# Query projection by halves of w_q, keys turned two blocks at a time, and one V load with uneven rows

## The chip, the cores and the metric

One Trainium2 chip, and one of its cores. The metric is device time in microseconds (us) of one execution of the whole kernel. Each NeuronCore has five engines that run side by side and wait for each other by semaphores: PE (TensorE, matmuls; PEld is its weight load), DVE (VectorE), ACT (ScalarE), POOL (GpSimd) and SP (SyncE, which here issues every transfer). Transfers from HBM to the on-chip memory (SBUF) run on 16 DMA engines.

## What is computed

Two layers of a decoder for four sequences with one new token each (x is 4 x 512), and each layer is an attention over cached keys and values and then a gated feed-forward block. Both layers read the same weights and the same caches. Cut to its core:

```python
# B=4, D=512, Hq=32, Hkv=8, Sk=8192, Dh=128, F=1792, all bf16
def attention(x, k_cache, v_cache, wq, wo):      # caches: B x Hkv x Sk x Dh
    q = (x @ wq) as B x Hq x 1 x Dh
    k, v = each of the 8 heads repeated for 4 query heads
    p = softmax(q @ k^T * Dh ** -0.5)
    return (p @ v) as B x 1 x 4096 @ wo
def ffn(x, w_gate, w_up, w_down):
    return (silu(x @ w_gate) * (x @ w_up)) @ w_down
for layer in range(2):
    x = x + attention(layernorm(x), ...)
    x = x + ffn(layernorm(x), ...)
```

## The kernel before

The caches of one layer are 128 MB. The kernel cuts them into 16 units, one per sequence and pair of key heads; a unit has 4 MB of keys (K) and 4 MB of values (V), each laid on 128 partitions (rows) of 32 KB. A row has 8 blocks of 4 KB (`NB = 8`, `BW` is the width of a block). Five slots of that size hold them: slots 0 to 3 and slot 4 (`QS`), whose place w_q has at the start of each layer. The second layer starts with units whose data the first has left in SBUF: K and V of unit 15 and V of unit 14 stay, and the last two blocks of K of unit 13 are parked in PSUM (`hold`) and brought back.

**Order of loads.** `cmds` (lines 349 to 364) is a fixed list of (what, slot, first block, last block). `pump` (L400) goes through it in order and issues the next load when all of its blocks are free; `freed` (L434) marks blocks as free when the step that reads them last has been written, and calls `pump`. All loads go through SP, which waits for the readers of the blocks before it issues (`load`, L419; L63 is the wait and L93 the issue in the profile). Most loads are a whole slot. Some are cut: `half` gives two of four blocks, `ends` gives blocks 0-3, 4-6 and 7. The first loads of layer 1 are K of its second unit (unit 14) into the slot where the feed-forward weights of layer 0 lie (slot 1, as blocks 0-2, 3 and 4-7, each when the weights there have been read), K of the third unit (unit 13) into slot 4 (blocks 0-3, 4-5), and then, from `seq`, K and V of the next, the first two in halves.

**Work on a unit.** `keys` (L598) turns each block of K on DVE (`turn`, L483, transpose on L488: 128 x 1024 fp32, in place) and then writes the scores of the block: four matmuls of 128 x 512 on PE (`scores`, L512). Then come the maximum (L518, L526), the exponentials on ACT (L559), the transpose of the probabilities (L576), and with V the products (`values`, L643), the gather on DVE (L689, L693) and the sums. Work of the next units is placed in between: the order of the instructions on each engine is written out by `blocks`, `line` and `drain`, with a rough cost for each step (0.9 for a block).

**The boundary between layers.** After the last V of layer 0: output projection (L784), layernorm (`center`, L807 to L821; `deviation`, L826), feed-forward (`ffn`: gate and up on L876, down on L907 for layer 0 in three parts of w_down, L897 for layer 1), layernorm again, and the query projection (`qproj`, L839). `qproj` has 128 matmuls of 4 columns: for each of the 32 heads four, over the four parts kt of w_q, of which two come from each half (`wq0`, `wq1`); `deviation` is written after half of the heads. Then `hold` brings the two parked blocks back into slot 4, and blocks 0-5 of slot 4 are freed.

**The end.** V of the last unit comes as blocks 0-3, 4-6 and 7. Behind it come the feed-forward weights of layer 1, and the last part of w_down when the place of the last probabilities is free.

Of the kernel before, what the change touches and what calls it, by code (L numbers as in the profile page):

```python
# [9 lines left out]
FP32 = mybir.dt.float32  # L10
# [93 lines left out]
def bass_interleave_layers__gqa_block_cached__swiglu_ffn__decode_kernel(  # L104
# [40 lines left out]
    with ExitStack() as es:  # L145
# [50 lines left out]
        def room(s, a, b):  # L196
            return [f"s{s}.{q}" for q in range(a // BW, (b - 1) // BW + 1)]
# [48 lines left out]
        def bank(k):  # L246
            return ps[:, k * BANKF:(k + 1) * BANKF]
# [87 lines left out]

        ends = lambda it, s: [(it, s, 0, QH), (it, s, QH, NB - 1), (it, s, NB - 1, NB)]
        half = lambda it, s: [(it, s, q, q + NB // 2) for q in range(0, NB, NB // 2)]

        def placed(seq, ring, parts):
            out = []  # L340
            for i, it in enumerate(seq):
                s = ring[i % len(ring)]
                out += parts[i](it, s) if i in parts else [(it, s, 0, NB)]
            return out
# [10 lines left out]

        us = order[1]
        s = W_SLOT[0]
        cmds += [(K(1, us[1]), s, 0, 3), (K(1, us[1]), s, 3, 4), (K(1, us[1]), s, 4, NB)]
        cmds += [(K(1, us[2]), QS, 0, NB // 2), (K(1, us[2]), QS, NB // 2, NB - 2)]
        seq = loads(1, 3)  # L360
        ring = (0, 1, 3, QS, 2)
        cmds += placed(seq, ring, {0: half, 1: half, len(seq) - 1: ends})
        assert W_SLOT[1] == ring[len(seq) % len(ring)]
        cmds += [(("W", 1), W_SLOT[1], 0, NB), (("W+", 1), W_SLOT[1], NB, NB + 1)]

# [55 lines left out]

        q_gone = set()

        def load(it, a, b, sm):
            kind, L, u = it
            s = slot_of[it]
            gp, bt = pair_gb(u)
            src = (A_k_cache if kind == "K" else A_v_cache)[bt, 2 * gp:2 * gp + 2, :, :].rearrange(
                "h (p t) d -> (h p) (t d)", t=TT)
            over = WQ if s == QS and not q_gone else []  # L430
            q_gone.update(over)
            T.dma("sp", kv[:, s, a * BW:b * BW], src[:, a * BW:b * BW], sm,
                  writes=[f"s{s}.{q}" for q in range(a, b)] + over)

        def freed(s, a, b):
            free.update((s, q) for q in range(a, b))
# [7 lines left out]
        def hold(q, back):  # L444
            s = QS if back else slot_of[half_kept]
            w = kv[:, s, q * BW:(q + 1) * BW].bitcast(FP32)
            k = STEP + 2 * (q - NB + 2)
            banks = ps[:, k * BANKF:(k + 2) * BANKF]
            here, there = [f"s{s}.{q}"], [f"pb{k}", f"pb{k + 1}"]
            if back:  # L450
                T._wait("dve", T._need((), WQ))
                T.op("dve", lambda e: e.transpose(w, banks), reads=there, writes=here)  # L452
                turned.add((1, NP - 3, q))
            else:
                T.op("dve", lambda e: e.transpose(banks, w), reads=here, writes=there)
            held[0] = not back or q < NB - 1
# [23 lines left out]
                line.pop(0)[2]()  # L480


        def turn(L, u, q):  # L483


            s = slot_of[K(L, u)]
            w = kv[:, s, q * BW:(q + 1) * BW].bitcast(FP32)
            T.op("dve", lambda e: e.transpose(w, w), reads=[f"s{s}.{q}"], writes=[f"s{s}.{q}"])  # L488
            turned.add((L, u, q))

        placed_q = set()

# [105 lines left out]
        def keys(L, u, before, lag):  # L598
            def block(q):
                if q == 0:  # L600
                    place_q(L, u)
                scores(L, u, q)
                finished(K(L, u), q, q + 1)
                if q == NB - 1:
                    step = lambda gap, fn: [gap, u, lambda: fn(u)]
                    line.extend([step(0.0, max_p), step(1.2, max_t)])
                    after = [step(0.9, exps), step(1.3, lambda u: turn_p(L, u))]
                    if u == order[L][-1]:
                        after = [after[0], step(0.3, lambda u: turn_p(L, u)), [2.5, None, lambda: total(u)]]
                    (line if before is None else behind.setdefault(before, [])).extend(after)  # L610

            drain(lag)
            for q in range(NB):
                if (L, u, q) not in turned:
                    turn(L, u, q)
                blocks.append((0.9, lambda q=q: block(q)))
                drain(lag)

# [213 lines left out]

        def qproj(L, u):
            at, name = place("ln", 0, Hq * B)
            for h in range(Hq):
                if h == Hq // 2:
                    deviation(lsc_sb, "lsc")
                for kt in range(KT):
                    T.op("pe", lambda e: e.matmul(at[:, h * B:(h + 1) * B],  # L839
                                                  lhsT=wq_sb[:, kt, h * Dh:(h + 1) * Dh],  # L840
                                                  rhs=xn[:, kt * B:(kt + 1) * B],
                                                  start=(kt == 0), stop=(kt == KT - 1)),
                         reads=[f"wq{kt // 2}", "xn"], writes=[name], sig=(kt == KT - 1))
            T.op("dve", lambda e: e.tensor_tensor(qT, at.rearrange("p (h b) -> p b h", b=B),
                                                  rstd[:].unsqueeze(2).to_broadcast([P, B, Hq]), ALU.mult),
                 reads=[name, "rstd"], writes=["qT"] + OT)

            pick = ident.rearrange("p (c j e) -> p c j e", c=2, e=2)
            ob, oname = place("q", 0, NQR)
            ob = ob.rearrange("p (c b g r) -> p c b g r", c=4, b=B, g=GP)  # L850
            qv = qT.rearrange("p b (g h r) -> p b g h r", h=2, r=REP)
            for c in range(4):
                for a in range(NA):
                    T.op("pe", lambda e: e.matmul(ob[a * QB:(a + 1) * QB, c],
                                                  lhsT=pick[:, c // 2, :, c % 2],
                                                  rhs=qv[:, :, :, a // 2, :], start=True, stop=True),
                         reads=["qT", "ident"], writes=[oname], sig=(a == NA - 1))
            place_q(L, u, "dve", ob, [oname])
            T.op("dve", lambda e: e.tensor_copy(qr, ob), reads=[oname], writes=["qr", "made"])

        def ffn(L):
# [3 lines left out]
            uT = bank(ub)[:, 0:FO * B]  # L865
            fb = lambda ap: ap.rearrange("p (f b) -> p f b", b=B)
            rb = rstd[:].unsqueeze(1).to_broadcast([P, FO, B])
            rooms = {"wg": room(s, 0, O_WU), "wu": room(s, O_WU, O_WD), "wd": room(s, O_WD, O_WD + FO * D)}
            names = {"wg": ["wg"], "wu": ["wu0", "wu1", "wu2"]}
            for at, wname, bk in ((wg_at, "wg", gb), (wu_at, "wu", ub)):  # L870
                for fo in range(FO):
# [19 lines left out]
            if L == 1:  # L891
                x_rows(1)
                for i, (a, b, _) in enumerate(WDS[1]):
                    for fo in range(a, b):
                        for j in range(NA):
                            o = s * SL + O_WD + fo * D + j * P
                            T.op("pe", lambda e: e.matmul(quarter(j), lhsT=hT[:, fo * B:(fo + 1) * B],  # L897
                                                          rhs=kvf[:, o:o + P], start=False, stop=(fo == FO - 1)),
                                 reads=["hT", f"wd{i}"] + rooms["wd"], writes=[f"part{j}"],
                                 sig=(fo == b - 1))  # L900
                freed(s, 4, NB)
                return
            for j, (a, b, _) in enumerate(WDS[0]):
                k = OBK[0] if j else SBK[1]
                for nt in range(KT):
                    for fo in range(a, b):
                        T.op("pe", lambda e: e.matmul(bank(k)[:, nt * B:(nt + 1) * B],  # L907
                                                      lhsT=wd_at(s, fo, nt),
                                                      rhs=hT[:, fo * B:(fo + 1) * B],
                                                      start=(j < 2 and nt == 0 and fo == a),  # L910
                                                      stop=(j in (0, NW - 1) and nt == KT - 1 and fo == b - 1)),
                             reads=["hT", f"wd{j}"] + rooms["wd"], writes=[f"pb{k}"], sig=(fo == b - 1))
                if not j:
                    add_to_x(bank(k)[:, 0:XB], f"pb{k}")
            freed(s, 4, NB)
            add_to_x(bank(k)[:, 0:XB], f"pb{k}")


# [10 lines left out]
        for L in range(2):  # L929
# [6 lines left out]
            if L:  # L936
                for q in (NB - 2, NB - 1):
                    hold(q, True)
                freed(QS, 0, NB - 2)
            todo = [("K", 0)]  # L940
            for i in range(1, NP - 1):
                todo += [("K", i), ("V", i - 1)]
# [49 lines left out]
```

## Time and profile before

| | us |
|---|---|
| median of 3 runs | 648.85 (648.73 to 649.52) |
| the profiled execution | 648.29 |
| its span, first to last instruction | 646.5 |
| busy in the span: PE | 425.6 (66%) |
| DVE | 430.1 (67%) |
| ACT | 41.2 (6%) |
| POOL | 11.1 (2%) |
| transfers | 273.37 MB, mean 423 GB/s |

The page of the profile gives busy times, the span in 40 slices of 16.2 us (a digit is the busy share in tenths; GB/s is what the DMA engines moved), the DMA queues, and groups of instructions by line: how often, how long in total, the mean in ns, and then how long the engine was idle just before them and what ended most of that idle time. A row of the timeline has the start, the time, engine, line, operation, output and input, how many instructions were merged, and in brackets the idle time before it and who ended it. The chain of waits follows the work that ended last back from the end of the kernel. q1 is the queue of the kernel's own transfers; q8 carries the program's instructions.

### The profile page before, as it was taken

Reading aid. Unit: us, or ns where it says so; the run is one execution under the profiler, and the core shown is the slowest. Engines: PE = TensorE matmul, PEld = TensorE weight load, DVE = VectorE, ACT = ScalarE, POOL = GpSimd, SP = SyncE. Lnnn points to the kernel's source line nnn. Section 1 sums busy time; section 2 is a strip of 40 time slices with the busy share of each in tenths; the row PEclk is TensorE's granted clock in tenths of the full one; section 3 lists DMA queues with packets and bytes.
Section 4 is the critical chain, followed back from the end, with each engine's and each line's share of the span. In section 5 each row is a group of like instructions: output and inputs, shape, how many; then the busy total and the mean of one; then the engine's idle time right before and its main releaser. Section 6 shows DMA issues by size and latency. Waiting matters only on the chain.

```text
span 646.5 us, 7503 instructions
## 1 busy us (share of the span) xinstructions
PE 425.6 (66%) x3128; PEld 173.1 (27%) x3128; DVE 430.1 (67%) x706; ACT 41.2 (6%) x117; POOL 11.1 (2%) x43
## 2 busy tenths in 40 slices
PE   2574466556766755767757987777665576657878
PEld 2221122212322212222226332222222222222225
DVE  1585467566776666777852878888766677766953
ACT  1000000000000000001010010000000000000110
POOL 0000000000000000000000000000000000000000
PEclk9996896789787999878985799999878997789977
DMA  9999999999999999999999999999999999999996
GB/s 363 445 423 416 442 429 430 426 435 433 426 430 435 430 425 436 435 422 436 434 407 409 396 435 434 434 429 423 442 427 426 433 438 424 431 440 423 430 417 268
DMA packets 14129, 273.37 MB, mean 423 GB/s; under 512 B 1416, under 2 KB 1424, under 8 KB 5264
## 3 DMA queue, kind: packets, MB, share of 16 engines
q1 hardware_dynamic: 14096, 272.91, 99.0%
q8 instruction: 24, 0.39, 0.2%
q14 instruction: 9, 0.07, 0.0%
HBM read 272.90 MB, written 0.00 MB: 422 GB/s over the span
## 4 chain that ended last, share of the span: by engine, by line
DMA 61%; DVE 26%; PE 9%; issue 3%; SPq 0%; ACT 0%; DVEq 0%
DMA kvf<-in_A_k_cache_dram 49%; DVE kvf L488 20%; DMA kvf<-in_A_v_cache_dram 10%; PE ps L512 3%; DVE pT L576 3%; PE ps L643 2%; DMA kvf<-in_B_w_down_dram 2%; DVE pb L693 2%; PE ps L839 1%; DVE pb L689 0%; PE ps L876 0%; DVE scr L703 0%; DVE kvf L452 0%; PE ps L759 0%; SPq L93 0%
## 5 line engine op out<-in xcount | busy, mean ns | idle before, releaser
L512 PE MATMUL ps<-kvf,zq 128*128 128x512 bf16 x1024 | 298.0, 426 | 181.1 <-DVE kvf L488 174.3
L488 DVE STREAM_TRANSPOSE kvf<-kvf 128x1024 f32<-128x1024 f32 x246 | 289.8, 1219 | 108.6 <-DMA kvf<-in_A_k_cache_dram 107.7
L512 PEld LDWEIGHTS ps<-kvf,zq 128*128 128x128 bf16 x1024 | 90.6, 105 | 350.9 <-DVE kvf L488 257.8
L643 PE MATMUL ps<-kvf,pT 128*32 128x512 bf16 x960 | 66.7, 400 | 1.4 <-DVE pT L576 0.8
L559 ACT ACTIVATE pb<-ps,tiny 128x512 bf16<-128x512 f32 x32 | 22.0, 688 | 531.8 <-DVE tiny L557 495.2
L576 DVE STREAM_TRANSPOSE pT<-pb 64x512 bf16<-64x512 bf16 x60 | 41.2, 687 | 3.1 <-ACT pb L559 2.0
L518 DVE TENSOR_REDUCE tiny<-ps 128x1 f32<-128x512 f32 x32 | 22.0, 687 | 31.6 <-PE ps L512 31.6
L693 DVE SCALAR_TENSOR_TENSOR pb<-ps,tiny,pb 128x128 f32<-128x128 f32 x104 | 36.5, 351 | 5.1 <-PE ps L643 1.3
L643 PEld LDWEIGHTS ps<-kvf,pT 128*32 128x32 bf16 x960 | 20.8, 98 | 31.9 <-issue 15.7
L698 PEld LDWEIGHTS ps<-sel,pb 128*128 128x128 f32 x64 | 15.4, 258 | 21.3 <-DVE pb L693 14.0
L502 POOL TENSOR_TENSOR zq<-scr,tiny 128x64 bf16<-128x64 bf16 x30 | 9.0, 300 | 564.8 <-PE ps L512 564.8
L526 DVE TENSOR_REDUCE mrm<-ps 1x8 f32<-1x128 f32 x32 | 8.8, 275 | 14.2 <-PE ps L523 14.2
L698 PE MATMUL ps<-sel,pb 128*128 128x8 f32 x64 | 12.7, 272 | 8.1 <-DVE pb L693 8.1
L549 PEld LDWEIGHTS ps<-mrm,tiny 128*128 128x128 f32 x60 | 12.0, 205 | 8.6 <-DVE scr L703 3.2
L759 PE MATMUL ps<-wo_sb,scr 128*4 128x512 bf16 x48 | 11.0, 379 | 1.5 <-DVE scr L728 1.5
L689 DVE TENSOR_SCALAR pb<-ps,tiny 128x128 f32<-128x128 f32 x32 | 10.1, 315 | 2.6 <-PE ps L643 2.6
L549 PE MATMUL ps<-mrm,tiny 128*128 128x16 f32 x60 | 9.3, 231 | 3.1 <-ACT mrm L561 3.1
L839 PE MATMUL ps<-xn,kvf 128*128 128x4 bf16 x256 | 7.6, 166 | 3.8 <-DMA kvf<-in_A_wq_dram 3.0
L561 ACT ACTIVATE mrm<-head,tiny 128x8 f32<-128x8 f32 x32 | 9.6, 301 | 1.0
L523 PE MATMUL ps<-identf,tiny 128*1 128x128 f32 x32 | 8.6, 270 | 0.2 <-DVE tiny L518 0.2
L839 PEld LDWEIGHTS ps<-xn,kvf 128*128 128x128 bf16 x256 | 7.6, 106 | 4.0 <-DMA kvf<-in_A_wq_dram 3.1
L876 PE MATMUL ps<-xn,kvf 128*128 128x4 bf16 x224 | 7.3, 169 | 1.8 <-DMA kvf<-in_B_w_up_dram 1.4
(83 smaller groups left out, 113.9 us busy)
## 6 DMA issues: line engine op xcount, KB each, us to landing
kvf<-in_A_k_cache_dram SPq DMA_DIRECT2D x28, 4096.0 KB, 30.8
kvf<-in_A_v_cache_dram SPq DMA_DIRECT2D x27, 4096.0 KB, 32.9
kvf<-in_A_v_cache_dram SPq DMA_DIRECT2D x4, 2048.0 KB, 20.0
kvf<-in_A_k_cache_dram SPq DMA_DIRECT2D x4, 2048.0 KB, 10.0
kvf<-in_A_wq_dram SPq DMA_DIRECT2D x2, 2048.0 KB, 9.8
wo_sb<-in_A_wo_dram SPq DMA_DIRECT2D x4, 1024.0 KB, 40.6
kvf<-in_B_w_gate_dram SPq DMA_DIRECT2D x2, 1792.0 KB, 24.5
kvf<-in_A_v_cache_dram SPq DMA_DIRECT2D x2, 1536.0 KB, 34.8
```

The costliest lines, as they stand in the source:

```text
L488: T.op("dve", lambda e: e.transpose(w, w), reads=[f"s{s}.{q}"], writes=[f"s{s}.{q}"])
L512: T.op("pe", lambda e: e.matmul(bank(bk)[:, 0:SW], lhsT=zq[:, z0:z0 + P], rhs=w[:, :, c // 2, :, c % 2], start=(q == 0 and c == 0), stop=( ...
L518: T.op("dve", lambda e: e.tensor_reduce(mx[:], bank(bk)[:, 0:SW], AX.X, ALU.max), reads=[f"pb{bk}"], writes=["mx"])
L549: T.op("pe", lambda e: e.matmul(at, lhsT=ones, rhs=mrm[:, i * H2:(i + 2) * H2], start=True, stop=True), reads=[f"m8{i}", "rsm", "onesf"], ...
L559: T.op("act", lambda e: e.activation(pb[:], bank(bk)[:, 0:SW], ACTF.Exp, bias=nm, accum_out=rs), reads=[f"pb{bk}", "nm"], writes=PB + ["rs"])
L576: T.op("dve", lambda e: e.transpose(dst, pb[hp]), reads=["pb", "row"], writes=[name])
L643: T.op("pe", lambda e: e.matmul(bank(k)[j * QB:(j + 1) * QB, q0 * Dh:q1 * Dh], lhsT=p_t[:, t, h, :], rhs=v[:, q0:q1, t, :], start=((last o ...
L689: T.op("dve", lambda e: e.tensor_scalar(into, o, own[:, q:q + 1], None, op0=ALU.mult), reads=[f"pb{k}", "own"], writes=["row"] if last els ...
L693: T.op("dve", lambda e: e.scalar_tensor_tensor(into, o, own[:, q:q + 1], into, op0=ALU.mult, op1=ALU.add), reads=[f"pb{k}", "own", iname], ...
L698: T.op("pe", lambda e: e.matmul(at, lhsT=into, rhs=sel[:], start=True, stop=True), reads=[iname, "sel"], writes=[name])
L759: T.op("pe", lambda e: e.matmul(bank(OUTB)[0:B, 0:D], lhsT=oT[:, h, :], rhs=wo_sb[:, h, :], start=(gp == groups[L][0] and r == 0), stop=(g ...
L839: T.op("pe", lambda e: e.matmul(at[:, h * B:(h + 1) * B], lhsT=wq_sb[:, kt, h * Dh:(h + 1) * Dh], rhs=xn[:, kt * B:(kt + 1) * B], start=(k ...
```

## The change

1. `qproj` runs over the two halves of w_q outside and the heads inside; `deviation` stands between the halves. In layer 1, blocks 0-3 of slot 4, where the first half of w_q lies, are freed after the first half.
2. The down projection reads its weights block by block (`rooms` for each part of w_down), so in layer 0 blocks 4 and 5 of slot 1 are freed after the first part. The load of K of the second unit of layer 1 is cut further, as blocks 0-2, 3, 4-5 and 6-7.
3. The first load of `seq` in layer 1 comes as four loads of two blocks (`twos`), not two of four.
4. DVE turns two blocks of K in one instruction (128 x 2048) in all units but the first and the last of a layer.
5. V of the tenth unit of layer 1 (unit 5) is cut into blocks 0-5 (24 KB of each row) and 6-7. The first of these is loaded as seven transfers: rows 1, 3, 5, ... (64 rows), rows 2, 6, 10, ... (32), rows 4, 12, 20, ... (16), and then the 16 rows that are left in four transfers of 4 rows (0, 32, 64, 96 and so on). All seven count up one semaphore.

```diff
         half = lambda it, s: [(it, s, q, q + NB // 2) for q in range(0, NB, NB // 2)]
+        twos = lambda it, s: [(it, s, q, q + 2) for q in range(0, NB, 2)]
...
-        cmds += [(K(1, us[1]), s, 0, 3), (K(1, us[1]), s, 3, 4), (K(1, us[1]), s, 4, NB)]
+        cmds += [(K(1, us[1]), s, a, b) for a, b in ((0, 3), (3, 4), (4, 6), (6, NB))]
...
-        cmds += placed(seq, ring, {0: half, 1: half, len(seq) - 1: ends})
+        cut = lambda it, s: [(it, s, 0, 6), (it, s, 6, NB)]
+        cmds += placed(seq, ring, {0: twos, 1: half, seq.index(V(1, us[9])): cut, len(seq) - 1: ends})
...
+        uneven = (V(1, order[1][9]), 0)
...
-            over = WQ if s == QS and not q_gone else []
+            over = [w for i, w in enumerate(WQ) if s == QS and a // (NB // 2) == i and w not in q_gone]
             q_gone.update(over)
-            T.dma("sp", kv[:, s, a * BW:b * BW], src[:, a * BW:b * BW], sm,
-                  writes=[f"s{s}.{q}" for q in range(a, b)] + over)
+            names = [f"s{s}.{q}" for q in range(a, b)] + over
+            rows = [slice(0, P)]
+            if (it, a) == uneven:
+                rows = [slice(i, P, m) for i, m in ((1, 2), (2, 4), (4, 8), (0, 32), (8, 32), (16, 32), (24, 32))]
+                T.wait_res("sp", writes=names)
+            for r in rows[:-1]:
+                T.dma("sp", kv[r, s, a * BW:b * BW], src[r, a * BW:b * BW], sm)
+            T.dma("sp", kv[rows[-1], s, a * BW:b * BW], src[rows[-1], a * BW:b * BW], sm, writes=names)
...
-                T._wait("dve", T._need((), WQ))
+                T._wait("dve", T._need((), WQ[1:]))
...
-        def turn(L, u, q):
-
-
+        def turn(L, u, q, n):
             s = slot_of[K(L, u)]
-            w = kv[:, s, q * BW:(q + 1) * BW].bitcast(FP32)
-            T.op("dve", lambda e: e.transpose(w, w), reads=[f"s{s}.{q}"], writes=[f"s{s}.{q}"])
-            turned.add((L, u, q))
+            w = kv[:, s, q * BW:(q + n) * BW].bitcast(FP32)
+            names = [f"s{s}.{i}" for i in range(q, q + n)]
+            T.op("dve", lambda e: e.transpose(w, w), reads=names, writes=names)
+            turned.update((L, u, i) for i in range(q, q + n))
...
                 if (L, u, q) not in turned:
-                    turn(L, u, q)
+                    two = 0 < order[L].index(u) < NP - 1 and q % 2 == 0 and (L, u, q + 1) not in turned
+                    turn(L, u, q, 1 + two)
...
-            for h in range(Hq):
-                if h == Hq // 2:
+            for c in range(2):
+                if c:
                     deviation(lsc_sb, "lsc")
-                for kt in range(KT):
...
+                for h in range(Hq):
+                    for kt in (2 * c, 2 * c + 1):
...
+                if L and not c:
+                    freed(QS, 0, NB // 2)
...
-            rooms = {"wg": room(s, 0, O_WU), "wu": room(s, O_WU, O_WD), "wd": room(s, O_WD, O_WD + FO * D)}
+            rooms = {"wg": room(s, 0, O_WU), "wu": room(s, O_WU, O_WD)}
+            for j, (a, b, _) in enumerate(WDS[L]):
+                rooms[f"wd{j}"] = room(s, O_WD + a * D, O_WD + b * D)
...
                 if not j:
+                    freed(s, 4, 6)
                     add_to_x(bank(k)[:, 0:XB], f"pb{k}")
-            freed(s, 4, NB)
+            freed(s, 6, NB)
...
-                freed(QS, 0, NB - 2)
+                freed(QS, NB // 2, NB - 2)
```

More of the change, by code (lines that the diff above doesn't have):

```diff
@@ L834, in qproj @@
             at, name = place("ln", 0, Hq * B)
-            for h in range(Hq):
-                if h == Hq // 2:
+            for c in range(2):
+                if c:
                     deviation(lsc_sb, "lsc")
-                for kt in range(KT):
[L839 to L843, printed above, removed]
+                for h in range(Hq):
+                    for kt in (2 * c, 2 * c + 1):
+                        T.op("pe", lambda e: e.matmul(at[:, h * B:(h + 1) * B],
+                                                      lhsT=wq_sb[:, kt, h * Dh:(h + 1) * Dh],
+                                                      rhs=xn[:, kt * B:(kt + 1) * B],
+                                                      start=(kt == 0 and h == 0), stop=(kt == KT - 1 and h == Hq - 1)),
+                             reads=[f"wq{c}", "xn"], writes=[name], sig=(kt % 2 == 1 and h == Hq - 1))
+                if L and not c:
+                    freed(QS, 0, NB // 2)
             T.op("dve", lambda e: e.tensor_tensor(qT, at.rearrange("p (h b) -> p b h", b=B),
@@ L898, in ffn @@
                                                           rhs=kvf[:, o:o + P], start=False, stop=(fo == FO - 1)),
-                                 reads=["hT", f"wd{i}"] + rooms["wd"], writes=[f"part{j}"],
+                                 reads=["hT", f"wd{i}"] + rooms[f"wd{i}"], writes=[f"part{j}"],
                                  sig=(fo == b - 1))
@@ L911, in ffn @@
                                                       stop=(j in (0, NW - 1) and nt == KT - 1 and fo == b - 1)),
-                             reads=["hT", f"wd{j}"] + rooms["wd"], writes=[f"pb{k}"], sig=(fo == b - 1))
+                             reads=["hT", f"wd{j}"] + rooms[f"wd{j}"], writes=[f"pb{k}"], sig=(fo == b - 1))
                 if not j:
+                    freed(s, 4, 6)
                     add_to_x(bank(k)[:, 0:XB], f"pb{k}")
-            freed(s, 4, NB)
+            freed(s, 6, NB)
             add_to_x(bank(k)[:, 0:XB], f"pb{k}")
```

## The prediction

> **What bounds the kernel now.** The page first: the span, what the transfers do, and the chain that ended last.
>
> ```profile
> span 646.5 us, 7503 instructions
> DMA  9999999999999999999999999999999999999996
> GB/s 363 445 423 416 442 429 430 426 435 433 426 430 435 430 425 436 435 422 436 434 407 409 396 435 434 434 429 423 442 427 426 433 438 424 431 440 423 430 417 268
> q1 hardware_dynamic: 14096, 272.91, 99.0%
> q8 instruction: 24, 0.39, 0.2%
> DMA 61%; DVE 26%; PE 9%; issue 3%; SPq 0%; ACT 0%; DVEq 0%
> L488 DVE STREAM_TRANSPOSE kvf<-kvf 128x1024 f32<-128x1024 f32 x246 | 289.8, 1219 | 108.6 <-DMA kvf<-in_A_k_cache_dram 107.7
> ```
>
> The 16 DMA engines are busy in every slice, and the bytes do not change. DVE, which the change relieves, waits 107.7 us for keys. So the time can only come from where a DMA engine is idle or where the engines finish unevenly. Two places: slices 20 to 22 (407, 409, 396 GB/s), the boundary between the two layers, and the end.
>
> Second view, busy time by windows (columns: PE, PEld, DVE, ACT, POOL, clock, DMA share, GB/s), and the SyncE queue at the boundary:
>
> ```profile
> 339.00:351.00 12.00, 8.24 (x221) 7.66 (x221) 3.07 (x15) 0.81 (x3) 0.00 (x0) 0.50 1.02 413
> 351.00:357.00 6.00, 4.75 (x138) 4.49 (x135) 1.25 (x7) 0.56 (x2) 0.00 (x0) 0.50 1.01 412
> 357.00:363.00 6.00, 5.63 (x29) 2.09 (x30) 5.50 (x7) 0.00 (x0) 0.00 (x0) 0.52 0.95 363
> 363.00:370.00 7.00, 6.24 (x29) 2.44 (x28) 6.93 (x7) 0.00 (x0) 0.30 (x1) 1.00 0.98 398
> 370.00:376.00 6.00, 6.00 (x31) 2.62 (x35) 1.92 (x6) 1.08 (x3) 0.00 (x0) 1.00 1.02 434
> ```
>
> Here loads are held up by compute: key loads go out at 345.06, 348.35, 351.19, 356.71, 357.08, 363.87 and 367.36 us, each when PE has read the slot.
>
> Third, the packets one by one. On a busy engine a packet starts 3 to 4 ns before the last one ends, so the packets can be strung into 16 engines. A 32 KB row takes 1.215 us. The 24 instruction packets of q8 fall in turn on the same eight engines ("fetching"), once per some 255 instructions of PE, and each sets its engine back by about 1.5 us; the other eight ("light") get none. (Strings in step may be swapped, inside a class.) Lateness behind the earliest engine, us, worked out from the packets:
>
> ```
> transfer ends at   eight light engines                      eight fetching engines
> 351.87 (K, 4 KB)   0.00 0.04 0.12 0.16 0.53 0.71 0.93 2.83  1.35 1.47 1.49 1.75 3.16 3.17 3.26 3.38
> 363.77 (K, 16 KB)  0.00 0.02 0.03 0.17 0.20 0.23 1.14 1.65  0.03 0.11 0.18 0.76 1.33 1.36 1.39 1.50
> 628.59 (last V)    0.00 0.22 0.34 0.80 1.45 1.50 1.67 4.07  1.84 2.47 2.86 2.91 2.92 2.98 3.03 4.59
> ```
>
> Between the first two rows the early engines ran dry and the late ones caught up. The last V ends when the slowest engine ends, 633.18, against a mean of 630.7. One light engine is late for another reason: three stalls of 0.97 us (385, 484, 597 us), one per some 128 DVE instructions.
>
> Last, the end:
>
> ```profile
> 593.19 2.37 DVE L488 STREAM_TRANSPOSE kvf<-kvf 128x1024 f32<-128x1024 f32 x2 [4.39 <-DMA kvf<-in_A_k_cache_dram]
> 623.86 2.75 PE L643 MATMUL ps<-kvf,pT 128*32 128x512 bf16 x24 [0.64 <-DVE tiny L557]
> 633.78 0.41 PE L643 MATMUL ps<-kvf 128*32 128x128 bf16 x16
> 643.85 0.10 PEld L897 LDWEIGHTS ps<-kvf,pb 128*4 128x4 bf16 x8 [0.17 <-DMA kvf<-in_B_w_down_dram]
> ```
>
> Compute waits for the last keys but one (593.19), for the last V (landing 633.7, PE at 633.78), and for the last of w_down (landing 643.8, PE at 643.85). Behind V there are 12.7 us of fixed work; the w_down transfer follows V on the same engines. Both move with the slowest engine.
>
> **The change part by part.**
>
> *Earlier loads at the boundary* (query halves, w_down by part, keys by twos of blocks). A load issued at 351.19 to a dry engine moved data from about 352.9 on: 1.75 us. On the earliest engine, with 0.152 us per 4 KB, eight rows each: K blocks 0-3 end at 351.87. Blocks 4, 5 now go out when the first w_down part is read (PE, 349.9), so data by 351.7, in time; they take 2.43 us, to 354.3. Blocks 6, 7 go out at 351.2, in time, to 356.7. The first half of slot 4 is free after 64 of the 128 query matmuls (352.64 + 1.87 = 354.5, instead of 356.71), data by 356.3, in time, to 361.6; two more blocks to 364.0. The next key comes by twos from about 360.8, 363.9, 365.6 and 367.4, always ahead of need, to 373.7; then V, issued at 372.50, is up to 0.5 us late for the earliest engines. So nearly all idling goes. What was it worth? Engines late by 3.16 to 3.38 us at 351.87 never ran dry and ended the last V at 631.45 to 631.62 with one more instruction packet: about 276.3 us, less 1.5 and 0.3 (a long packet at 359-361, when the others restart), or 274.6 us of plain transfers. Without idling the seven early light engines would end at 626.5 to 627.4 (were 628.6 to 630.3), fetching ones near 631.3. The latest of all, 633.18, sat 2.2 us dry (long first packets at 358.2 and 366.3) and is worth that much.
>
> *16 rows in four transfers of four.* One row of 24 KB is 0.91 us. The first three transfers (64, 32, 16 rows) give each engine 7 rows; the others give four engines 4 more, if they spread as x did: x has 4 rows, its semaphore saw 5 updates instead of 16, and its four packets sat on four engines, at least three of them light, probably all. So twelve engines gain 0.91 us and four lose 2.73. Six more transfers cost 4-byte packets of 9 ns and SyncE issues of about 0.4 us (0.33 to 0.49 in the trace), with 20 us of queue ahead: nothing.
>
> [...]
>
> *Keys turned in twos.* 246 transposes become 135. A double one is not in the trace: from 64x512 bf16 (687 ns) to 128x1024 (1219 ns) the slope is 1.04 ns per element, so 2283 ns; the bounds are 2438 (two singles) and 2130 (slope alone). Back to back that saves about 0.07 us a pair; the first block of a pair is ready 1.1 us later, under loads issued 20 us ahead (8 us at the start). I take 0; uncovered it costs 1 us once. Fewer DVE instructions (787 to 676 records) should also drop the third 0.97 us stall (at record 706); I do not count on it.
>
> *Query halves in layer 0* start at 8.5 instead of 13.4 us: nothing, DMA is the bound there.
>
> **Sum.** End of the last V: fetching engines 355.25 + 274.6 + 1.5 - 0.9 = 630.5, or with two packets to come 353.6 + 274.6 + 3.1 - 0.9 = 630.4; four loaded engines 626.5 to 627.4 + 2.73 = 629.2 to 630.1, plus up to 0.5; the stalled light engine 354.7 + 274.6 + 2.9 - 0.9 = 631.3 (630.3 without its third stall). Latest 631.3, before 633.18: **-1.9 us**. The keys that gate DVE at 593.19 come 1.2 us earlier, and behind them PE has 0.4 to 0.9 us to spare at each V part, so compute allows about -2.1. W_down: 631.3 + 10.1 = 641.4 instead of 643.3, -1.9. The profiled execution took 648.29 (span 646.5 and 1.8 around it), 0.56 below the median; I take the difference from the median: 648.85 - 1.9 = **646.9 us**.
>
> **Rivals.**
> 1. *The idling only moves* (V at 372.50, or DVE holds the end): the fetching engines keep their place, the rows alone give 0.9 to 1.2: 647.8. For it: DVE works without a break from 593 to 616. Against: all issue times above are ahead of need. 0.16.
> 2. *The four-row transfers spread over all engines*: nothing is shifted, only the boundary helps: 632.2 instead of 633.18, 647.9. Against: x's five updates. 0.07.
> 3. *Slower: the four engines are not early.* Whoever ended later than 633.18 - 2.73 = 630.45 becomes the last. If a fetching engine is among them: 630.5 + 0.9 + 2.7 = 634.1, +0.9: 649.8; if all four rows go to one engine, 16 x 0.91 = 14.6 on it, +8 and more. For it: one of the four packets of x may belong to a fetching engine. 0.10.
>
> [...]
>
> **Numbers.** Forecast 0.67, its own range 645.9 (third stall gone, compute free) to 647.5. A measurement of this kernel tells about 0.2%, 1.3 us: faster below 647.55, slower above 650.15. Cases 1 and 2 (0.23) and a fifth of case 3 (0.02) lie within. Faster 0.67, same 0.25, slower 0.08. Range 645.8 to 648.6.
>
> **What would show it.** Slices 20 to 22 near 430 GB/s; key loads at about 350, 354.5 and 361; engines at the last V within 1.5 us of each other except one; last V at PE by 632. Wrong if four engines end 2 us behind the others, if the early engines still restart with long packets after 366, or if DVE no longer waits for keys near 592.

## The result and the profile after

| | before | after |
|---|---|---|
| median, us | 648.97 (648.73 to 649.52, 4 runs) | 656.87 (656.47 to 657.19, 4 runs) |
| ratio | | 1.0122, 95% interval 1.0109 to 1.0135 |
| profiled execution, span, us | 646.5 | 654.8 |
| last V at PE, us | 633.78 | 641.65 |

The change makes the kernel 7.9 us slower, where 646.9 was forecast. The page of after, the same lines as before:

```profile
span 654.8 us, 7425 instructions
DMA  9999999999999999999999999999999999999994
GB/s 377 423 431 415 438 441 416 439 424 435 428 434 428 427 436 425 438 424 440 417 411 416 422 435 439 421 441 421 442 419 445 327 398 430 433 427 431 430 412 154
q1 hardware_dynamic: 14720, 272.91, 98.4%
L497 DVE STREAM_TRANSPOSE kvf<-kvf 128x2048 f32<-128x2048 f32 (+1 forms) x135 | 280.3, 2102 | 133.6 <-DMA kvf<-in_A_k_cache_dram 133.4
```

Two things are to be read here. Slices 20 to 22 now carry 411, 416 and 422 GB/s instead of 407, 409 and 396: the boundary between the layers is better filled. But slice 31 (counted from 0, as 20 to 22 are), which had 433, has 327, and the next has 398 instead of 438. The row of busy tenths shows nothing of it: a DMA engine whose packets take twice as long is as "busy" as before (a share of 1.05 at 282 GB/s from 516 to 528 us, where before has 1.00 at 429). Only the bytes tell. DVE's wait for keys rises from 107.7 to 133.4 us, but this is no measure of the loss: the version with whole rows (e1 below), which is faster than before, has 129.4.

Busy time by windows (stretch, its length, then PE, PEld, DVE, ACT, POOL, the granted clock, the DMA share, GB/s). The first two answer to the rows of before at 363 and 398 GB/s; the others are new:

```profile
357.00:363.00 6.00, 5.65 (x30) 2.11 (x18) 5.77 (x6) 0.00 (x0) 0.00 (x0) 0.64 1.02 426
363.00:370.00 7.00, 5.94 (x28) 2.33 (x26) 6.64 (x5) 0.00 (x0) 0.30 (x1) 1.00 0.99 417
510.00:516.00 6.00, 0.61 (x12) 0.11 (x4) 0.58 (x1) 0.00 (x0) 0.00 (x0) 0.91 0.94 396
516.00:528.00 12.00, 9.53 (x36) 3.90 (x36) 11.28 (x14) 1.08 (x3) 0.00 (x0) 0.76 1.05 282
528.00:534.00 6.00, 2.17 (x22) 0.55 (x25) 0.97 (x2) 0.00 (x0) 0.30 (x1) 0.83 0.94 386
```

From 516 to 528 us the core gets 282 GB/s with every engine busy. This is where the V load of 24 KB with uneven rows passes (its first packet starts at 510.59). Put together from the packets, per microsecond: how much moved, and by packet size the mean number of engines on it and the GB/s of one engine on it.

```
us    GB/s   24 KB packets       8 KB (rest of that V)   32 KB (next load)
515   425    16.1 at 26.4
516   354    16.0 at 22.1
518   251    12.0 at 15.5         4.1 at 15.9
520   249    12.0 at 15.5         4.1 at 15.4
522   199     7.4 at 12.9         5.2 at 11.6             3.4 at 12.9
524   235     4.8 at 14.4         7.2 at 14.5             4.0 at 15.2
526   362     1.0 at 16.1         7.9 at 22.7             7.2 at 23.1
529   367     1.0 at 14.7                                15.0 at 23.4
531   428                         1.0 at 26.2            15.1 at 26.7
```

Through the transfers of 64 and 32 rows a packet of 24 KB takes the 0.91 us that the prediction worked out. When the first engines have reached the transfer of 16 rows, it takes 1.5 to 2.1 us, and everything else slows with it: 8 KB packets take 0.4 to 0.75 us instead of 0.31, and 32 KB packets of the next load up to 2.8 us instead of 1.215. At the end a single engine is left on rows of the transfers of four (14.7 GB/s), and the other 15, which have ordinary rows, still run at 23.4 instead of 27.

The timeline (start, time, engine, line, operation, in brackets the wait and who ended it) at the places that were shown of before:

```profile
602.54 2.31 DVE L497 STREAM_TRANSPOSE kvf<-kvf 128x2048 f32<-128x2048 f32 x1 [5.99 <-DMA kvf<-in_A_k_cache_dram]
...
633.37 2.75 PE L653 MATMUL ps<-kvf,pT 128*32 128x512 bf16 x24 [0.57 <-DVE pT L585]
...
641.65 0.23 PEld L653 LDWEIGHTS ps<-kvf 128*32 128x32 bf16 x16 [0.42 <-DMA kvf<-in_A_v_cache_dram]
```

The keys that DVE had at 593.19 come at 602.54, and the last V is at PE 7.87 us later. So what waits for loads behind the V load comes 7.9 to 9.4 us later. Lateness of the engines at the end of the last V, worked out from the packets as in the prediction (the earliest ends at 630.93):

```
0.00 0.15 0.43 0.74 2.67 3.57 3.96 4.01 4.09 4.17 4.22 4.34 4.42 4.94 5.05 10.11
```

The mean end of the 16 engines is 634.5, where it was 630.7 before. So there are two losses: the engines are late by 3.8 us in the mean, and one of them ends 5 us behind the next.

### The profile page after: what moved, and what is told of

It reads as the page before. It is cut to its first block, busy times and chain, and to the rows that moved or that the text cites. A ratio compares the mean times of both kernels' runs of the same rounds, so it can differ in the third digit from the quotient of the medians.

```text
span 654.8 us, 7425 instructions
## 1 busy us (share of the span) xinstructions
PE 420.0 (64%) x3128; PEld 181.3 (28%) x3128; DVE 422.0 (64%) x595; ACT 41.2 (6%) x117; POOL 11.1 (2%) x43
## 4 chain that ended last, share of the span: by engine, by line
DMA 55%; DVE 24%; PE 13%; issue 4%; another core or an unknown queue 3%; SPq 1%; ACT 0%; POOL 0%; ACTq 0%; POOLq 0%; DVEq 0%
DMA kvf<-in_A_k_cache_dram 43%; DVE kvf L497 18%; DMA kvf<-in_A_v_cache_dram 10%; PE ps L521 7%; PE ps L653 3%; DVE pb L703 2%; DMA kvf<-in_B_w_down_dram 2%; SPq L93 1%; DVE pb L699 1%; DVE pT L585 1%; PE ps L850 1%; PE ps L891 0%; DVE scr L713 0%; DVE kvf L462 0%
## 5 line engine op out<-in xcount | busy, mean ns | idle before, releaser
L521 PE MATMUL ps<-kvf,zq 128*128 128x512 bf16 x1024 | 294.5, 434 | 197.3 <-DVE kvf L497 193.5
L497 DVE STREAM_TRANSPOSE kvf<-kvf 128x2048 f32<-128x2048 f32 (+1 forms) x135 | 280.3, 2102 | 133.6 <-DMA kvf<-in_A_k_cache_dram 133.4
L521 PEld LDWEIGHTS ps<-kvf,zq 128*128 128x128 bf16 x1024 | 99.8, 108 | 355.6 <-DVE kvf L497 237.1
```

Of the source, the lines that this page charges most:

```text
L497: T.op("dve", lambda e: e.transpose(w, w), reads=names, writes=names)
L521: T.op("pe", lambda e: e.matmul(bank(bk)[:, 0:SW], lhsT=zq[:, z0:z0 + P], rhs=w[:, :, c // 2, :, c % 2], start=(q == 0 and c == 0), stop=( ...
```

## The experiments

The kernel before ran beside each group; ratios are to it, in brackets the 95% interval.

| label | what | median, us | ratio |
|---|---|---|---|
| e1_whole_rows | the change, 24 KB part in one transfer | 647.29 | 0.9979 [0.9971, 0.9988] |
| e2_rows_alone | before, with the seven transfers alone | 658.02 | 1.0144 [1.0128, 1.0159] |
| e3_rows_112 | the change, 112 rows and four times 4 | 662.25 | 1.0211 [1.0197, 1.0225] |
| e4_even_strided | the change, 64, 32, 16 and 16 rows | 652.34 | 1.0059 [1.0046, 1.0073] |
| e5_two_32 | the change, 64, 32 and 32 rows | 647.36 | 0.9979 [0.9970, 0.9989] |
| e6_16_from_neighbours | e4, 16 rows read side by side in HBM | 651.86 | 1.0049 [1.0036, 1.0063] |
| e7_32_from_every_8th | e5, last 32 rows read eight apart | 647.33 | 0.9978 [0.9969, 0.9987] |
| e8_turn_singles | e1, keys turned one by one | 648.14 | 0.9993 [0.9984, 1.0002] |
| e9_twos_alone | before, keys turned in twos | 648.08 | 0.9992 [0.9983, 1.0001] |
| e10_eight_rows | the change, 64, 32 and four times 8 | 653.48 | 1.0081 [1.0067, 1.0095] |

### Which part costs it: e1 and e2

```
e1   -            if (it, a) == uneven:
     +            if (it, a) == uneven and False:
e2   the kernel before, with
     +        cut = lambda it, s: [(it, s, 0, 6), (it, s, 6, NB)]
     +  ... seq.index(V(1, us[9])): cut ...   and the change's load()
```

> The change without its uneven rows: the V load stays cut into 24 KB and 8 KB columns, each with all 128 rows in one transfer. If the seven transfers cost all of the loss, packets of 24 KB take 0.91 us throughout and the last V ends at about 632.0 (earliest engine 510.6 + 116.7, latest 4.7 behind it) instead of 633.2: 647.7 us, 1.2 below before. If keys in twos or the earlier loads cost something as well, it stays above 649.5.

> The kernel before with the cut and the seven transfers alone. If they carry the whole loss: 655 to 658 us, and 24 KB packets of 1.5 us and more between the second transfer and the end of the four-row ones. If the loss needs the rest of the change: below 651.

E1 took 647.29 against 648.41, 1.1 us less (ratio 0.9979). E2 took 658.02: 9.6 us slower. So the seven transfers are the whole loss, and the rest of the change is a small gain. Windows of e1, then of e2:

```profile
357.00:363.00 6.00, 5.51 (x30) 2.08 (x31) 5.47 (x7) 0.00 (x0) 0.00 (x0) 0.57 1.01 422
516.00:528.00 12.00, 9.40 (x35) 4.06 (x36) 11.56 (x14) 1.08 (x3) 0.00 (x0) 0.73 1.02 435
```

```profile
517.00:528.00 11.00, 9.62 (x32) 3.92 (x32) 10.79 (x18) 1.08 (x3) 0.00 (x0) 0.72 1.01 230
```

E1 has the filled boundary (422) and no dip; e2 has the dip without anything else of the change. In this dip the whole core is at about half its rate for 11 us (230 GB/s; before, the packets move 431 to 433 in each microsecond from 518 to 532), and not only the four engines that take four rows more.

### Pattern, number or concentration: e3 and e4

```
e3   rows = [slice(0, 112)] + [slice(112 + j, P, 4) for j in range(4)]
e4   rows = [slice(i, P, m) for i, m in ((1, 2), (2, 4), (4, 8), (0, 8))]
```

> The change with the same loads per engine, but as 112 neighbouring rows in one transfer and then four transfers of rows four apart (112, 116, 120, 124 and so on). If only the pattern of the strided rows slows the packets, they take about 0.91 us here, and only the three rows more on the engine that stalls by 0.97 us now and then show: last V at about 634.7, 650.4 us. If any transfer that puts rows on four engines slows all packets: 655 to 658.

> The change with the strided transfers of 64, 32 and 16 rows, and the 16 left over as one transfer of 16 rows (0, 8, 16 ...): eight rows on every engine again. If the concentration on four engines slows the packets: none slower than 1 us, 647.7 us. If the strided pattern does it: packets of 1.5 us and more from the second transfer on, some 3 to 5 us lost on every engine, 651 to 653.

E3 was meant to be the cure: as many rows per engine as in the change, but the bulk as one block without a stride. It is the worst of all, 13.8 us slower than before, and outside both times that I expected. E4 gives every engine the same eight rows, so nothing is concentrated, and is slow too. Windows of e3:

```profile
512.00:520.00 8.00, 0.00 (x0) 0.00 (x0) 0.62 (x1) 0.00 (x0) 0.00 (x0) 0.61 0.96 208
520.00:533.00 13.00, 10.31 (x36) 4.39 (x36) 12.05 (x15) 1.08 (x3) 0.30 (x1) 0.72 1.02 228
```

and of e4:

```profile
510.00:516.00 6.00, 0.65 (x12) 0.11 (x4) 0.48 (x1) 0.00 (x0) 0.00 (x0) 0.90 0.97 408
516.00:528.00 12.00, 9.35 (x36) 3.90 (x36) 11.39 (x14) 1.08 (x3) 0.00 (x0) 0.77 1.01 261
```

In e3 the half rate starts with the block of 112 rows, before any engine has come to the transfers of four (the 112 rows, seven for each of 16 engines, are ahead of them), and it starts when only one to six engines have reached it: the others, still on the ordinary 32 KB rows of the load ahead, fall from 27 to 13.5 to 15 GB/s as well. In e4 the 64 and 32 rows are at 408 GB/s, and the two transfers of 16 rows at 261. My theory up to here, that four engines with four rows each made the packets slow, fell with e4; that it was the stride fell with e3.

### Read side or write side: e5, e6 and e7

What sets 16 and 112 rows apart from 128, 64 and 32 could be the number of rows in a transfer, the distance of the rows in HBM (16 rows eight apart are 256 KB apart; the 112 rows lie side by side), or the rows of SBUF that an engine writes.

```
e5   rows = [slice(i, P, m) for i, m in ((1, 2), (2, 4), (0, 4))]
e6   e4, and   froms[2:] = [src[0:16, ...], src[16:32, ...]]
e7   e5, and   froms[2] = wide[0:2 * P:8, ...]
```

> Strided rows, eight on each engine: transfers of 64, 32 and again 32 rows (0, 4, 8 ...), none of 16. In the runs so far packets stayed at 0.91 us through the 64-row and 32-row transfers and slowed when the first engines reached one of 16 rows. If it is the 16-row transfer (its rows fall on engines otherwise than in whole loads): no packet above 1 us, 647.3 us like the version with whole rows. If it is the strided or small transfers as such: 650 and more.

> As the version with 64, 32, 16 and 16 rows (652.3 us), but the two 16-row transfers read the first 32 rows of the unit in HBM as neighbours, and write the same SBUF rows 8 apart as before (the V of this unit is so permuted, and its part of the attention with it). If the SBUF rows an engine writes decide: slow packets again, 652.3. If the 256 KB pitch of the reads in HBM decides: 647.3.

> The counterpart: 64, 32 and 32 rows written to SBUF in the pattern that stayed fast, but the last 32 are read from every 8th row of HBM, over two units (V of this unit is partly that of its neighbour, and its part of the attention with it). If the SBUF rows decide: 647.3 us, no packet above 1 us. If the pitch of the reads decides: slow packets, 650 to 652.

The same window of each, first e5, then e6, then e7:

```profile
516.00:528.00 12.00, 9.27 (x36) 3.83 (x36) 11.40 (x14) 1.08 (x3) 0.00 (x0) 0.77 1.02 434
```

```profile
516.00:528.00 12.00, 9.74 (x36) 4.12 (x36) 11.40 (x14) 1.08 (x3) 0.00 (x0) 0.72 1.00 264
```

```profile
516.00:528.00 12.00, 9.82 (x34) 4.27 (x35) 11.74 (x14) 1.08 (x3) 0.00 (x0) 0.66 1.03 441
```

Three transfers of strided rows cost nothing (e5, 434 GB/s, the same time as e1). Sixteen rows that are neighbours in HBM, written eight rows apart, are as slow as before (264). Thirty-two rows that lie 256 KB apart in HBM, written four rows apart, run at 441. The read side is out. These three runs leave two things that go together in them: the rows of SBUF, and the number of rows in a transfer (16 are slow, 32 are not). E10, below, takes them apart.

Half of the 432 GB/s of an undisturbed stretch would be 216. E4 and e6 come near it from above (261 and 264 over windows that hold the start and the end of the dip; 249 to 252 from 518 to 521 us in after), and e3 had 208. That the rows of a 16-row transfer fall on engines otherwise than those of a whole load I assumed; no run shows which engine writes which row.

### Four transfers of eight rows: e10

```
rows = [slice(1, P, 2), slice(2, P, 4)] + [slice(o, o + 29, 4) for o in (0, 32, 64, 96)]
```

> The change with 64 and 32 strided rows, and the other 32 (0, 4, 8 ...) as four transfers of 8 rows: 0 to 28, 32 to 60, 64 to 92, 96 to 124. Eight engines then take ten rows and eight take six. [...] Rival (any small transfer on fewer than 16 engines slows all): slow from the first 8-row transfer on, 651 and more.

Its windows, cut where the packets change:

```profile
514.00:516.00 2.00, 0.00 (x0) 0.00 (x0) 0.59 (x1) 0.00 (x0) 0.00 (x0) 0.50 0.97 418
516.00:517.80 1.80, 0.02 (x1) 0.02 (x2) 1.80 (x2) 0.00 (x0) 0.00 (x0) 0.50 0.93 396
517.80:520.00 2.20, 2.20 (x6) 0.79 (x7) 2.10 (x5) 0.00 (x0) 0.00 (x0) 0.50 1.31 328
520.00:528.00 8.00, 7.97 (x32) 3.55 (x30) 7.50 (x9) 1.08 (x3) 0.00 (x0) 0.76 0.99 247
```

The window counts a packet where it starts; spread over their time, the packets move 430 and 426 GB/s in the microseconds at 516 and 517. On the engines that come first the packets took 0.91 to 0.93 us through the transfers on rows 0 to 28 and 32 to 60; when these engines reach the third, rows 64 to 92, all 24 KB packets take 1.07 to 1.86 us. All four transfers have eight rows, four apart, so neither the number of rows nor their spacing makes the difference: which rows of SBUF are written does. I had put the run at 647.5 to 650 us, with about 3 us of slow packets from the third transfer on; that the rows from 64 on would be the slow ones I assumed, and no run had shown it. The packets went that way, but the time missed, 653.48 instead of at most 650; it fell into the range of the rival (651 and more), whose other sign, slow packets from the first of the four transfers on, did not come. I had counted the half rate for as long as the first engines need for their packets. It lasts until the last of the eight engines, which are late ones too, is through: 517.8 to 528.3, some 10 us.

### What the rest is worth: e8 and e9

```
e8   e1, and   two = 0
e9   the kernel before, with the change's turn() and two
```

> The version with whole rows (ratio 0.998 to before), with each key block turned by itself as before. If the earlier loads at the boundary carry its gain: the same ratio, 0.997 to 0.999. If the keys turned in twos carry it: 0.9995 to 1.001; if twos cost something, below 0.997.

> The kernel before with nothing but keys turned in twos. Theory: it saves the third 0.97 us stall of one DMA engine, which is worth something only when that engine ends last. In the kernel before an engine that fetches instructions ends last (633.2 against 632.7), so ratio 0.999 to 1.0005 here, and the gain of twos in the version with whole rows needs the earlier loads beside it. Rival: twos gain 0.0014 by themselves (less work on DVE near the end): 0.9985 or lower.

Each alone is 0.07 or 0.08% faster, and neither interval is clear of 1; e8 lies between its two expected ranges. Together (e1) they give 0.21%, and e5 and e7, which have both and ran beside e8, lie 0.8 us under it. The sum of the two, 0.15%, lies inside the interval of e1 (0.12 to 0.29%), so the times do not show that one needs the other. Windows of the boundary, first e8, then e9:

```profile
357.00:363.00 6.00, 5.65 (x30) 2.08 (x31) 5.56 (x7) 0.00 (x0) 0.00 (x0) 0.55 1.03 430
```

```profile
357.00:363.00 6.00, 5.65 (x29) 2.08 (x30) 5.55 (x6) 0.00 (x0) 0.00 (x0) 0.51 0.99 390
```

The latest engine and its 0.97 us stalls show what the twos add once the boundary is filled (worked out from the packets, one trace of each; a stall is named by the start of its long packet, and comes once per some 128 DVE instructions, at DVE records near 450, 578 and 706):

```
kernel   DVE records   stalls at, us     boundary 357-363   last V ends on the latest engine
before   787           385 484 598       363 GB/s           633.18
e8       786           385 484 598       430 GB/s           632.92
e1       675           440 579           422 GB/s           631.98
```

Before, a fetching engine that had run dry at the boundary is last. When the boundary is filled (e8), the light engine with the stalls is last, 0.3 us earlier. Only when the twos take its third stall as well (e1) does the end move by 1.2 us. With the twos alone (e9) the boundary is as empty as before (390 and 398 GB/s in the two windows), and the last V lands at 632.9 instead of 633.7. My theory for e9, a fetching engine that stays last so that the saved stall gains nothing, is not borne out by this trace, though the ratio lies in the range that I gave; the rival's 0.9985 lies inside the interval too.

## Why the prediction was wrong

**Earlier loads at the boundary: right in kind, too large in size.** The key loads that I put at about 350, 354.5 and 361 us went out at 349.63, 354.31 and 361.14, and the window 357 to 363 rose from 363 to 426 GB/s. Slices 20 to 22 rose less than to 430, but from 349 to 376 us only 8 packets took more than 1.4 times their usual time, where 27 did before. Its worth, with my own terms and no uneven rows, would be a latest engine at 631.3 + 0.9 = 632.2, or -1.0 us. E1 gave -1.1, and its latest engine ended at 631.98, but that agreement is luck: e1 also has the saved stall, which I had put at 0. With the earlier loads alone (e8) the last engine ended at 632.92, 0.3 us earlier than before, and the median fell by 0.6 us, with an interval that touches 1.

**16 rows in four transfers of four: the step that failed.** I wrote that "twelve engines gain 0.91 us and four lose 2.73" and that six more transfers cost "nothing". The measured price of the step is 9.3 to 9.6 us: from 647.29 (e1) to 656.87 (after) and from 648.41 to 658.02 (e2) it is 9.6 by the medians, and 9.3 by the ratios of after and e1 to the kernel before. It failed in two places.

First, the duration. I took 0.91 us for a packet of 24 KB from rows of 128-row loads and carried it over to the same bytes on other rows. Here the price of a packet depends on which rows are written: 0.91 us in e1 and e5, 1.5 to 2.1 in after. With the shortfall against 432 GB/s summed over 516 to 531 us, 2,114 GB/s times 1 us, all engines lose 2,114 / 432 = 4.9 us; the mean end of the engines at the last V moves from 629.8 (e1, 15 engines that could be followed) to 634.5, 4.7 us, which agrees. E4, where every engine has eight rows, shows this half by itself: 652.34 - 647.29 = 5.05 us. The other half is the one engine that ends 5 us behind the rest: it ends 641.04 - 634.5 = 6.6 us after the mean, where e1's latest ends 631.98 - 629.8 = 2.2 us after it, 4.4 us more. Its last four packets took 1.67, 1.52, 1.66 and 1.67 us.

Second, the engines. X's five updates told rightly that four engines would take the rows: the semaphore of the seven transfers counts 3 x 16 + 4 x 5 = 68. That they are light held too: only one engine is on 24 KB packets after 525 us, and a fetching engine, which starts on them over 2 us behind the seven early light ones, would have been. But one of them was the light engine with the stalls, which I had as a term of its own at 631.3 with 0.91 us taken off. At the old packet time it would have ended at 631.3 + 0.91 + 2.73 = 634.9, 1.7 us later than the last engine of before (some 0.7 us later without its third stall, which the twos took away). This is my third rival, which I gave 0.10, with another engine than the one I named. So by its own terms the forecast would have missed even without the half rate. My sign for this case, four engines that end 2 us behind the others, came in another form: one ends 5 us behind.

**A split by itself.** E5 splits the load in three at no cost (647.36 against 647.29 in e1), so a split is not dear by itself; after, e3, e4, e6 and e10 pay for the rows chosen.

**Keys turned in twos: 0 was too little.** A double transpose takes 2295 ns, where I worked out 2283. I named the third stall and did not count on it. It went (675 records), and was worth about 0.8 us once the boundary was filled (e5 and e7 against e8). **Query halves in layer 0:** no gain was seen, and none was forecast; they were not tried alone.

**What stays open.** No run shows why the rate falls to about half, or why engines on ordinary rows are slowed as well: 13.5 to 15 GB/s in e3 with at most six engines on the 112 rows, and 23.4 in after with one engine left. Nor does any run show which engine writes which row of a transfer: the trace has engines only as strings of packets.

The best version is e1 (e5 and e7 are equal): the change without uneven rows, 0.2% faster than before.

## What to carry to other kernels

Here work could not be shifted between DMA engines by giving some of them more rows. A load with 16 rows eight apart, with 112 rows, or with eight rows of the far half halved the rate of all transfers (208 to 264 of 432 GB/s), those of other loads too, while several engines were on it, and cost some 15% of it while one was left (367 of 432 GB/s in after). When a load is to be cut, cut it in columns (435 GB/s in e1), or in sets of rows whose pattern ran at full rate (here 64 rows two apart and 32 rows four apart, 434 in e5). And where the busy share says 9 in every slice, read the bytes: of the two rows on DMA only the one in GB/s showed the loss.

## What the runs showed of the hardware that was not expected

- The rate went with the rows of SBUF that the transfers wrote: 434 to 441 GB/s for 64, 32 and 32 rows, 247 to 264 for 16 rows eight apart or eight of the rows 64 to 124, 208 to 228 for 112 rows.
- The slowdown is shared. While one engine was left on such rows at 14.7 GB/s, 15 others, on ordinary rows, ran at 23.4 instead of 27.
- One DMA engine stalled for 0.97 us once per some 128 DVE instructions (before: at DVE records 449, 578 and 706). Fewer DVE instructions (675 records in e1, 786 in e8) took one stall away, and with the boundary filled this was worth about 0.8 us (e5 and e7 against e8).
